# Weight blocks of K and Q loaded in joint pieces at the start of a one-core attention and feed-forward kernel

## The chip, the core and the metric

The kernel runs on one core of a Trainium2 chip. The metric is the device time of one execution in microseconds (us). The kernel before has a median of 210.56 us over 3 runs, which lie between 210.55 and 210.59 us.

## The reference

Input `x` has 2048 rows (tokens) of 512 numbers in bf16. The result is the sum of the input, a linear attention block and a feed-forward block, both applied to the normalised input:

```python
xn = _layernorm(x, axis=-1)
return x + _A_ref(xn, A_wqkv, A_wo) + _B_ref(xn, B_w_gate, B_w_up, B_w_down)

# A: qkv = xn @ wqkv (512 x 1536), 32 heads of 16
phi = lambda t: jnp.where(t > 0, t + 1, jnp.exp(t)) + 1e-6
pq, pk = phi(q), phi(k)
kv = einsum("bhsd,bhse->bhde", pk, v); z = einsum("bhsd->bhd", pk)
o = einsum("bhqd,bhde->bhqe", pq, kv) / (einsum("bhqd,bhd->bhq", pq, z)[..., None] + 1e-6)
# then o @ wo (512 x 512)
# B: (silu(xn @ w_gate) * (xn @ w_up)) @ w_down, inner width 1792
```

`wqkv` is one matrix of 512 rows and 1536 columns: columns 0 to 511 make Q, 512 to 1023 make K and 1024 to 1535 make V. So one row of it holds Q's 1 KB of weights directly ahead of K's 1 KB.

## The kernel before, in words

**Tiles.** The 2048 tokens are 16 tiles of 128. The width of 512 is 4 blocks (c = 0 to 3) of 128, since TensorE (PE) sums over 128 at a time. So K of one tile is four products, one per block of `xcT` (the centred input, transposed) and of the weights, summed in one bank of PSUM; `wk` c and `wq` c name the weights of block c for K and Q. A product of 128 x 128 by 128 x 512 is called a product below.

**Order.** Nothing is planned by a tool: the program is a list per engine, written out by hand, and every engine does its list in order. A helper (`_Prog`) records for each tile name who wrote it last, and adds the semaphore waits. A DMA signals when it has landed whole; every reader of any part of it waits for that. Loads are issued by SyncE (SP) and ScalarE (ACT), each from its own queue of DMAs; an ACT load stands in the same list as ACT's arithmetic.

**The start.** PE is kept running with five products of constants. Tiles 0 and 1 are transposed on PE raw (`traw`) and their mean is taken off there by a further product (`tcorr`); tile 0's mean comes from half sums (`sum_dve`, L388) in the kernel before already, and stays so. Tile 2 is centred on VectorE (DVE; `bns`, `agg`, two `xc_half`), transposed on PE (`tp_first`), and copied out by ACT (`tc_first`). Tile 3 is centred on DVE (`xc_full`) and transposed by a DMA (`transpose_xc`). The division by the standard deviation comes later, as a scale in ACT's `first_ek` (exponential of K), `first_pk` (positive part of K) and `first_pq` (Q).

**K and Q of tiles 0 and 1** (`proj_part`, L543) are written out product by product, in an order that follows the arrival of the weight blocks. K of tile 0 lies in bank 0, its Q in bank 1, K of tile 1 in bank 2, its Q in bank 3. Tile 2's `proj_first` (L530) uses banks 0 and 1 again and so waits for ACT's reads of them; tile 3 does with banks 2 and 3. ACT's list at this place is: `first_ek(0)`, `first_pk(0)`, `xn_act(0)`, two `tc_first(2)`, `first_pq(0)`, `first_ek(1)`, `first_pq(1)`, `first_pk(1)`. DVE's list is: `bns(2)`, `agg(2)`, two `xc_half(2)`, `bns(3)`, `agg(3)`, `clip_k(0)`, `xc_full(3)`, `bns(4)` and on with the statistics of tiles 5 and 6.

**After that** tiles 4 to 15 run in a loop (K, Q, their features, and the product of `xn` with the features of K, `gtacc`, L668), and then the feed-forward block (L870), with the output of four tiles worked in for each quarter of it (L1064, L1075).

**Loads of the start, before.** SP issues x 0, wk 0 and 1 (one DMA), wk 2, x 2, wq 0, wq 1, x 3, wq 2 and 3 (one DMA), x 4 and 5, x 6 and 7. ACT issues x 1 and wk 3. All weight loads read rows of 1 KB; x 4 and 5, and x 6 and 7, read rows of 2 KB, as there a partition takes two neighbouring tokens. A tile of x and a weight block are 128 KB each.

Of the kernel before, what the change touches and what calls it, by code (L numbers as in the profile page):

```python
# [10 lines left out]
P = 128  # L11
S = 2048
D = 512
# [96 lines left out]
def bass_parallel_sum__linear_attn_block__swiglu_ffn__prompt_kernel(  # L110
# [12 lines left out]
    K = _Prog()  # L123
    pe, act, dve, pool, sp = nc.tensor, nc.scalar, nc.vector, nc.gpsimd, nc.sync
    bf, f32 = dt.bfloat16, dt.float32

    with contextlib.ExitStack() as es:
        E = es.enter_context

        def sb(name, shape, d=bf):  # L130
            return E(nc.sbuf_tensor(name, [P] + shape, d))
# [7 lines left out]
        wqkv_sb = sb("wqkv_sb", [NDC, 3 * D])  # L139
# [16 lines left out]
        warm = sb("warm", [1], f32)  # L156
# [38 lines left out]
        def bk(i):  # L195
            return ("bank", i)
# [5 lines left out]
        def rows(v, t0, n):  # L202
            if t0 < NLONE:
                return v[t0 * P:(t0 + n) * P, :].rearrange("(t p) d -> p t d", p=P)
            return v[NLONE * P:, :].rearrange("(p t) d -> p t d", t=NT - NLONE)[:, t0 - NLONE:t0 - NLONE + n, :]

        def xload(eng, h, t0, n, after=()):
            K.dma(
                eng, lambda: h.dma_start(x_sb[:, t0:t0 + n, :], rows(xin, t0, n)),  # L209
                r=list(after), w=[("x", t0 + i) for i in range(n)],  # L210
            )

        def wqkv_load(eng, h, name, i, c0, n, after=()):
            K.dma(
                eng,
                lambda: h.dma_start(  # L216
                    wqkv_sb[:, c0:c0 + n, i * D:(i + 1) * D],
                    A_wqkv[c0 * P:(c0 + n) * P, i * D:(i + 1) * D].rearrange("(c p) f -> p c f", p=P),
                ),
                r=list(after), w=[(name, c) for c in range(c0, c0 + n)],  # L220
            )

        def wload(eng, h, name, dst, src):
            K.dma(eng, lambda: h.dma_start(dst[:, :, :], src.rearrange("(c p) f -> p c f", p=P)), w=[(name,)])

# [26 lines left out]

        xload("sp", sp, 0, 1)
        wqkv_load("sp", sp, "wk", 1, 0, 2)
        wqkv_load("act", act, "wk", 1, 3, 1)
        wqkv_load("sp", sp, "wk", 1, 2, 1)
        xload("sp", sp, 2, 1)
        wqkv_load("sp", sp, "wq", 0, 0, 1)
        wqkv_load("sp", sp, "wq", 0, 1, 1)
        xload("sp", sp, 3, 1)  # L260
        wqkv_load("sp", sp, "wq", 0, 2, 2)
        xload("sp", sp, 4, 2)
        xload("sp", sp, 6, 2)

# [34 lines left out]
        def bns(t):  # L299
            K.op("dve", lambda: dve.bn_stats(stats[:, t, :], x_sb[:, t, :]), r=[("x", t)], w=[("st", t)])  # L300

        def agg(t):
            K.op("dve", lambda: dve.bn_aggr(mv[:, t, :], stats[:, t, :]), r=[("st", t)], w=[("mv", t)])
# [155 lines left out]
        def tcopy(t, c0, n, b, eng):  # L459
            src, dst = banks[b][:, 0:n * P].rearrange("p (c s) -> p c s", c=n), xcT[:, NDC * t + c0:NDC * t + c0 + n, :]  # L460
            r, w = [bk(b)], [("xcT", t, c0 + i) for i in range(n)]
            if eng == "act":
                K.op("act", lambda: act.activation(dst, src, ACT.Copy), r=r, w=w)
            else:
                K.op("dve", lambda: dve.tensor_copy(dst, src), r=r, w=w)
# [10 lines left out]
        def transpose_xc(t):  # L476
            K.dma(
                "sp",
                lambda: sp.dma_start_transpose(out=xcT[:, NDC * t:NDC * (t + 1), :], in_=xc_sb[:, t, :]),
                r=[("xc", t, 0), ("xc", t, 1)], w=[("xcT", t, c) for c in range(NDC)],  # L480
            )
# [43 lines left out]
        def proj_first(t, wname, h):  # L525
            lo, b = (D, kb(t)) if wname == "wk" else (0, qb(t))
            K.op(
                "pe",
                [
                    (lambda c=c: pe.matmul(  # L530
                        banks[b], xcT[:, NDC * t + c, :], wqkv_sb[:, c, lo:lo + D],
                        start=(c == 0), stop=(c == NDC - 1),
                    ))
                    for c in (2 * h, 2 * h + 1)
                ],
                r=[("xcT", t, i) for i in (2 * h, 2 * h + 1)] + [(wname, i) for i in (2 * h, 2 * h + 1)], w=[bk(b)],
            )

        def proj_part(t, wname, c, pos):
            lo, b = (D, kb(t)) if wname == "wk" else (0, qb(t))  # L540
            K.op(
                "pe",
                lambda: pe.matmul(  # L543
                    banks[b], xcT[:, NDC * t + c, :], wqkv_sb[:, c, lo:lo + D],
                    start=(pos == 0), stop=(pos == NDC - 1),
                ),
                r=[("xcT", t, c), (wname, c)], w=[bk(b)],
            )

        def kb(t):  # L550
            return 2 * (t % 2)

        def qb(t):
            return 2 * (t % 2) + 1
# [43 lines left out]
        def first_ek(t):  # L598
            K.op(
                "act", lambda: act.activation(ek[:, t % NE, :], banks[kb(t)], ACT.Exp, scale=rstd[:, t:t + 1]),  # L600
                r=[bk(kb(t)), ("rstd", t)], w=[("ek", t % NE)],
            )

        def first_pk(t):
            K.op(
                "act", lambda: act.activation(kpos[:, t % NE, :], banks[kb(t)], ACT.Relu, scale=rstd[:, t:t + 1]),
                r=[bk(kb(t)), ("rstd", t)], w=[("kpos", t % NE)],
            )
# [7 lines left out]
        def first_pq(t):  # L616
            K.op(
                "act", lambda: act.activation(pkq[:, t, 1, :], banks[qb(t)], ACT.Identity, scale=rstd[:, t:t + 1]),
                r=[bk(qb(t)), ("rstd", t)], w=[("pq", t)],
            )  # L620
# [100 lines left out]
        proj_part(0, "wk", 1, 1)  # L721
        tcorr(1, 2, 3)
        tcopy(1, 2, 2, 3, "act")
        proj_part(0, "wk", 3, 2)
        proj_part(0, "wk", 2, 3)
        first_ek(0)
        clip_k(0)
        xc_full(3)
        bns(4)
        proj_part(1, "wk", 0, 0)  # L730
        proj_part(1, "wk", 1, 1)
        proj_part(1, "wk", 3, 2)
        proj_part(1, "wk", 2, 3)
        proj_part(1, "wq", 0, 0)
        proj_part(1, "wq", 1, 1)
        transpose_xc(3)
        xload("sp", sp, 8, 2)
        xload("sp", sp, 10, 2)
        proj_part(0, "wq", 0, 0)
        proj_part(0, "wq", 1, 1)  # L740
        first_pk(0)
        xn_act(0)
        tp_first(2, 0, 4)
# [5 lines left out]
        agg(5)  # L749
        bns(6)  # L750
        agg(6)
        proj_part(0, "wq", 2, 2)
        proj_part(1, "wq", 2, 2)
        proj_part(0, "wq", 3, 3)
        first_pq(0)
        proj_part(1, "wq", 3, 3)
        proj_first(2, "wk", 0)
        proj_first(2, "wk", 1)
        eps_two(1, "pool")
# [63 lines left out]
        for t in range(5, NT):  # L823
            kproj(t)
            exp_k(t)
            qproj(t)
            exp_q(t)
            copy_q(t)
            for i in XN0.get(t, ()):
                xn(i)  # L830
            feat_k(t)
            for i in STAT.get(t, ()):
                stat(i)
            for i in XN.get(t, ()):
                xn(i)
            if t in (6, 7, 8, 9):
                transpose_dma((3, 0, 1, 2)[t - 6])
            if t == 10:
                whalf("wg", wg_sb, B_w_gate, 0)
                whalf("wu", wu_sb, B_w_up, 0)  # L840
                wqkv_load("sp", sp, "wv", 2, 0, 4)
                wload("sp", sp, "wo", wo_sb, A_wo)
                whalf("wg", wg_sb, B_w_gate, 1)
            if t in (11, 12, 13, 14):
                late_eq(t - 11)
            if t == 12:
                masks()
            if t >= 12:
                gtacc(t - 2)
            elif t < 11:  # L850
                gtacc(t - 1)
# [260 lines left out]
        z_cols()  # L1112
        whalf("wu", wu_sb, B_w_up, 1)
        wload("sp", sp, "wd", wd_sb, B_w_down)
        NORM0 = 9
        PE_OUT = {3: 0, 6: 1, 9: 2, 12: 3}
# [56 lines left out]
```

## Time and profile before

| | before |
|---|---|
| median of 3 runs | 210.56 us (210.55 to 210.59) |
| the profiled execution | 210.56 us |
| its span, first to last instruction | 209.3 us |
| lies around the span | 1.26 us |
| PE busy | 205.0 us, 98% of the span |
| DVE, ACT, POOL busy | 119.7, 71.8, 72.2 us |
| granted TensorE clock | 1.00 |

All terms below come from this one profiled execution; its time is that of the median. Times are counted from the start of the span. A row of the timeline holds start, duration, engine, line, operation, output<-input and count; in brackets stands the idle time ahead of it and who ended it. "SPq" and "ACTq" are DMA issues; their duration is that of the issue, not of the transfer. "PEld" is PE's loading of the 128 x 128 operand, ahead of the product. A product is shown with 379 ns, but back-to-back ones start every 216 ns, since they overlap.

### The profile page before, as it was taken

The page shows a single profiled execution, that of the slowest core. Times are in us where ns is not written, and L with a number is a line of the kernel's source. Part 1 is how long each engine was busy: PE and PEld are TensorE (multiplying, and loading weights), DVE is VectorE, ACT ScalarE, POOL GpSimd, SP SyncE. Part 2 cuts the span into 40 slices and gives each one's busy share as a digit, 9 for nine tenths or more (in the row PEclk, how much of TensorE's full clock was granted, in tenths as well). Part 3 has the DMA queues.
Part 4 walks back from the last instruction along what each step waited for, and adds up shares of the span by engine and source line. Part 5 has one row for each costly group of instructions (what it writes and reads, how often), then busy time and mean ns, then how long its engine had stood idle before and what let it go on. Part 6 is the DMA issues. An engine that isn't in the chain of part 4 may idle for free.

```text
span 209.3 us, 2809 instructions
## 1 busy us (share of the span) xinstructions
PE 205.0 (98%) x998; PEld 94.5 (45%) x1017; DVE 119.7 (57%) x245; ACT 71.8 (34%) x127; POOL 72.2 (34%) x91
## 2 busy tenths in 40 slices
PE   8999999999999999999999999999999999999996
PEld 4444444444444444444444444444444444444444
DVE  4799988336365874637355746365556545374122
ACT  6877666966643331312112312213031213121000
POOL 2537987668032543223041422240424132221200
PEclk9999999999999999999999999999999999999999
DMA  6765645894696011010201110102011010110201
GB/s 197 219 184 79 127 100 102 258 364 153 206 356 49 11 39 25 28 25 25 52 0 50 28 28 22 50 0 53 5 45 25 25 28 28 49 27 27 53 25 50
DMA packets 30127, 16.84 MB, mean 80 GB/s; under 512 B 20896, under 2 KB 29344, under 8 KB 30112
## 3 DMA queue, kind: packets, MB, share of 16 engines
q1 hardware_dynamic: 29824, 16.39, 30.0%
q10 hardware_dynamic: 288, 0.26, 0.4%
q8 instruction: 8, 0.13, 0.2%
q14 instruction: 7, 0.06, 0.1%
HBM read 9.70 MB, written 2.10 MB: 56 GB/s over the span
## 4 chain that ended last, share of the span: by engine, by line
PE 91%; DVE 3%; DMA 2%; SPq 1%; issue 1%; POOL 1%; DVEq 0%
PE psum L870 44%; PE psum L1075 23%; PE psum L516 9%; PE psum L1064 7%; PE psum L668 6%; DMA wqkv_sb<-in_A_wqkv_dram 2%; PE psum L530 2%; SPq L216 1%; DVE pkq L592 1%; SPq L209 1%; POOL prod L1019 1%; PE psum L543 0%; DVE xn_sb L317 0%; DVE den L1027 0%; DVE pkq L891 0%
## 5 line engine op out<-in xcount | busy, mean ns | idle before, releaser
L885 ACT ACTIVATE sg<-psum 128x512 bf16<-128x512 f32 x56 | 33.4, 599 | 106.0 <-PE psum L870 103.6
L870 PE MATMUL psum<-xnT,wg_sb 128*128 128x512 bf16 x222 | 57.2, 379 | 0.2 <-issue 0.2
L870 PE MATMUL psum<-xnT,wu_sb 128*128 128x512 bf16 x216 | 55.8, 379 | 0.4
L1019 POOL TENSOR_TENSOR prod<-pkq,zb 128x512 f32<-128x512 bf16 x16 | 18.6, 1163 | 55.9 <-DVE pkq L592 55.9
L870 PEld LDWEIGHTS psum<-xnT,wu_sb 128*128 128x128 bf16 x224 | 21.9, 98 | 26.4
L870 PEld LDWEIGHTS psum<-xnT,wg_sb 128*128 128x128 bf16 x224 | 21.7, 98 | 26.2 <-issue 0.2
L1088 DVE TENSOR_TENSOR out_sb<-psum,x_sb 128x512 bf16<-128x512 f32 (+2 forms) x17 | 11.2, 661 | 36.2 <-PE psum L1075 36.2
L1043 POOL TENSOR_TENSOR pqn<-pkq,rden 128x512 bf16<-128x512 bf16 x16 | 16.9, 1058 | 36.6 <-DVE rden L1037 36.6
L891 DVE TENSOR_TENSOR pkq<-psum,sg 128x512 bf16<-128x512 f32 x28 | 19.2, 686 | 17.1 <-PE psum L870 14.6
L891 DVE TENSOR_TENSOR xn_sb<-psum,sg 128x512 bf16<-128x512 f32 x28 | 18.8, 672 | 13.8 <-PE psum L870 13.3
L1075 PE MATMUL psum<-wd_sb,xn_sb 128*128 128x512 bf16 (+2 forms) x126 | 25.7, 355 | 0.0
L1075 PE MATMUL psum<-wd_sb,pkq 128*128 128x512 bf16 x108 | 25.1, 379 | 0.2
L516 PE MATMUL psum<-wqkv_sb,xnT 128*128 128x512 bf16 x95 | 22.5, 379 | 0.1
L660 POOL TENSOR_TENSOR zacc<-zacc,pkq 128x512 f32<-128x512 f32 x15 | 17.4, 1157 | 5.0 <-DVE ek L583 4.6
L1075 PEld LDWEIGHTS psum<-wd_sb,xn_sb 128*128 128x128 bf16 x126 | 11.8, 98 | 12.5
L1075 PEld LDWEIGHTS psum<-wd_sb,pkq 128*128 128x128 bf16 x112 | 11.0, 98 | 13.2
L1064 PE MATMUL psum<-m_sb,eq 128*128 128x512 bf16 (+2 forms) x67 | 16.4, 366 | 0.1
L668 PE MATMUL psum<-pkq,xn_sb 128*128 128x512 bf16 x61 | 15.6, 379 | 0.2
L516 PEld LDWEIGHTS psum<-wqkv_sb,xnT 128*128 128x128 bf16 x96 | 9.4, 98 | 11.3
L1027 DVE TENSOR_REDUCE den<-prod 128x32 f32<-128x512 f32 x16 | 10.9, 684 | 5.9 <-POOL prod L1019 5.9
L300 DVE BATCH_NORM_STATS2 stats<-x_sb 128x6 f32<-128x512 bf16 x16 | 10.9, 680 | 1.1 <-DMA x_sb<-in_A_x_dram 1.1
L592 DVE SCALAR_TENSOR_TENSOR pkq<-pkq,eq 128x512 bf16<-128x512 bf16 x16 | 11.1, 692 | 0.6
(78 smaller groups left out, 139.7 us busy)
## 6 DMA issues: line engine op xcount, KB each, us to landing
out_dram<-out_sb SPq DMA_DIRECT2D x15, 128.0 KB, 1.7
wg_sb<-in_B_w_gate_dram SPq DMA_DIRECT2D x2, 896.0 KB, 7.5
wu_sb<-in_B_w_up_dram SPq DMA_DIRECT2D x2, 896.0 KB, 5.9
wd_sb<-in_B_w_down_dram SPq DMA_DIRECT2D x1, 1792.0 KB, 11.1
x_sb<-in_A_x_dram SPq DMA_DIRECT2D x6, 256.0 KB, 3.2
wqkv_sb<-in_A_wqkv_dram SPq DMA_DIRECT2D x2, 256.0 KB, 3.6
wqkv_sb<-in_A_wqkv_dram SPq DMA_DIRECT2D x1, 512.0 KB, 7.7
wo_sb<-in_A_wo_dram SPq DMA_DIRECT2D x1, 512.0 KB, 8.7
```

The lines of the kernel that those rows point to most:

```text
L516: (lambda c=c: pe.matmul(banks[b], xnT[:, c, t * P:(t + 1) * P], wqkv_sb[:, c, lo:lo + D], start=(c == 0), stop=(c == NDC - 1),))
L592: lambda: dve.scalar_tensor_tensor(out=dst, in0=src, scalar=0.0, in1=e, op0=ALU.max, op1=ALU.add,),
L660: lambda: pool.tensor_tensor(out=zacc[:, :], in0=zacc[:, :], in1=pk, op=ALU.add),
L668: (lambda c=c: pe.matmul(banks[4 + c], xn_sb[:, t, c * P:(c + 1) * P], pkq[:, t, 0, :], start=(t == 0), stop=(t == NT - 1),))
L870: (lambda c=c: pe.matmul(banks[b], w_sb[:, c, fc * P:(fc + 1) * P], xnT[:, c, C * 512:(C + 1) * 512], start=(c == 0), stop=(c == NDC - 1),))
L885: lambda: act.activation(sg[:, j % NSG, :], banks[gb], ACT.Silu),
L891: lambda: dve.tensor_tensor(out=hT(C, fc), in0=banks[ub], in1=sg[:, j % NSG, :], op=ALU.mult,),
L1019: lambda: pool.tensor_tensor(out=p, in0=pkq[:, t, 1, :], in1=zb[:, :], op=ALU.mult),
L1043: lambda: pool.tensor_tensor(out=pqn[:, t % NPN, :].rearrange("p (i g h e) -> p g i h e", i=NB, g=NG, e=DH), in0=pkq[:, t, 1, :].rearrange ...
L1064: (lambda g=g: pe.matmul(dst, pqnT(t)[:, g, :], m_sb[:, g, lo:hi], start=(g == 0), stop=False,))
L1075: (lambda fc=fc: pe.matmul(dst, hT(C, fc)[:, jj * P:(jj + 1) * P], wd_sb[:, fc, lo:hi], start=False, stop=(fc == NFC - 1),))
L1088: lambda: dve.tensor_tensor(out=o, in0=src, in1=x_sb[:, t, lo:hi], op=ALU.add),
```

## The change

A new function `qk_load` reads one block's rows over columns 0 to 1023, so Q's and K's weights of that block come in one DMA of 256 KB, in rows of 2 KB. It is used for blocks 2 and 3. Blocks 0 and 1 stay as they were for K (one DMA), and Q's blocks 0 and 1 become one DMA, issued behind x 3. The load of x 2 goes from SP's to ACT's queue, with a wait for ACT's first activation (`warm`); wk 3 leaves ACT's queue. Loads of the start are 10 in place of 12, with the same bytes.

The products of tiles 0 and 1 are put in another order: K of tile 0 takes blocks 0, 1, 2, then tile 1's K takes blocks 0 and 1, then tile 0's block 3 closes its K, then tile 1's blocks 2 and 3. Q takes blocks 2 and 3 of both tiles first and blocks 0 and 1 last. Their number is the same.

```diff
+        def qk_load(eng, h, c):
+            K.dma(
+                eng,
+                lambda: h.dma_start(wqkv_sb[:, c, 0:2 * D], A_wqkv[c * P:(c + 1) * P, 0:2 * D]),
+                w=[("wk", c), ("wq", c)],
+            )
...
         xload("sp", sp, 0, 1)
         wqkv_load("sp", sp, "wk", 1, 0, 2)
-        wqkv_load("act", act, "wk", 1, 3, 1)
-        wqkv_load("sp", sp, "wk", 1, 2, 1)
-        xload("sp", sp, 2, 1)
-        wqkv_load("sp", sp, "wq", 0, 0, 1)
-        wqkv_load("sp", sp, "wq", 0, 1, 1)
+        xload("act", act, 2, 1, [("warm",)])
+        qk_load("sp", sp, 2)
+        qk_load("sp", sp, 3)
         xload("sp", sp, 3, 1)
-        wqkv_load("sp", sp, "wq", 0, 2, 2)
+        wqkv_load("sp", sp, "wq", 0, 0, 2)
         xload("sp", sp, 4, 2)
         xload("sp", sp, 6, 2)
...
         proj_part(0, "wk", 1, 1)
         tcorr(1, 2, 3)
         tcopy(1, 2, 2, 3, "act")
-        proj_part(0, "wk", 3, 2)
-        proj_part(0, "wk", 2, 3)
+        proj_part(0, "wk", 2, 2)
+        proj_part(1, "wk", 0, 0)
+        proj_part(1, "wk", 1, 1)
+        proj_part(0, "wk", 3, 3)
+        proj_part(1, "wk", 2, 2)
+        proj_part(1, "wk", 3, 3)
         first_ek(0)
         clip_k(0)
         xc_full(3)
         bns(4)
-        proj_part(1, "wk", 0, 0)
-        proj_part(1, "wk", 1, 1)
-        proj_part(1, "wk", 3, 2)
-        proj_part(1, "wk", 2, 3)
-        proj_part(1, "wq", 0, 0)
-        proj_part(1, "wq", 1, 1)
+        proj_part(0, "wq", 2, 0)
+        proj_part(0, "wq", 3, 1)
         transpose_xc(3)
         xload("sp", sp, 8, 2)
         xload("sp", sp, 10, 2)
-        proj_part(0, "wq", 0, 0)
-        proj_part(0, "wq", 1, 1)
+        proj_part(1, "wq", 2, 0)
+        proj_part(1, "wq", 3, 1)
         first_pk(0)
...
-        proj_part(0, "wq", 2, 2)
-        proj_part(1, "wq", 2, 2)
-        proj_part(0, "wq", 3, 3)
+        proj_part(0, "wq", 0, 2)
+        proj_part(0, "wq", 1, 3)
+        proj_part(1, "wq", 0, 2)
         first_pq(0)
-        proj_part(1, "wq", 3, 3)
+        proj_part(1, "wq", 1, 3)
```

## The prediction

> **What bounds the kernel now.** I read the page's busy times first, then PE's waits, the chain of work that ended last, and then the first 16 us of the timeline.
>
> ```profile
> PE 205.0 (98%) x998; PEld 94.5 (45%) x1017; DVE 119.7 (57%) x245; ACT 71.8 (34%) x127; POOL 72.2 (34%) x91
> ...
> PE psum L543 <- DMA wqkv_sb<-in_A_wqkv_dram: 0.5, 1, 0.5
> PE psum L870 <- issue: 0.2, 1, 0.2
> ...
> 4.12 4.19 DMA wqkv_sb<-in_A_wqkv_dram
> 8.36 1.04 PE psum L543 x4
> ```
>
> PE is the bound. Once it has begun at 8.36 us it goes on back to back to the end, but for 0.2 us; the only wait before that worth a name is 0.5 us for a weight DMA, wq 2 and 3, issued at 4.12. So the change moves the end by as much as it moves PE's unbroken run, and by any new stall that it puts into the run. It cannot gain much more than the 0.5 us: ahead of 8.36 PE is busy.
>
> The loads that set that start, in order of issue (SP's, then ACT's with the activation `warm`):
>
> ```profile
> 0.80 0.40 SPq L209 DMA_DIRECT2D x_sb<-in_A_x_dram  x1
> 1.26 0.92 SPq L216 DMA_DIRECT2D wqkv_sb<-in_A_wqkv_dram  x2
> 2.23 0.43 SPq L209 DMA_DIRECT2D x_sb<-in_A_x_dram  x1
> 2.70 0.91 SPq L216 DMA_DIRECT2D wqkv_sb<-in_A_wqkv_dram  x2
> ...
> 4.12 0.44 SPq L216 DMA_DIRECT2D wqkv_sb<-in_A_wqkv_dram  x1
> ...
> 1.10 0.42 ACTq L209 DMA_DIRECT2D x_sb<-in_A_x_dram  x1
> 1.56 0.45 ACTq L216 DMA_DIRECT2D wqkv_sb<-in_A_wqkv_dram  x1
> 2.09 0.20 ACT L239 ACTIVATE warm<-warm 128x1 f32<-128x1 f32 x1
> ```
>
> And the instructions that date the landings: the first product is the first to use wk 3, the second to use wk 2; the others were released by a landing. The last row is of the view of the weights' tile for the issue at 1.26 alone: wk 0 and 1 land 3.0 us on, at 4.26.
>
> ```profile
> 5.28 2.36 PE L543 MATMUL psum<-wqkv_sb,xcT 128*128 128x512 bf16 x10
> 6.08 0.69 DVE L300 BATCH_NORM_STATS2 stats<-x_sb 128x6 f32<-128x512 bf16 x1 [0.76 <-DMA x_sb<-in_A_x_dram]
> 6.45 0.10 PEld L543 LDWEIGHTS psum<-wqkv_sb,xcT 128*128 128x128 bf16 x1 [0.21 <-DMA wqkv_sb<-in_A_wqkv_dram]
> 6.82 0.33 PEld L543 LDWEIGHTS psum<-wqkv_sb,xcT 128*128 128x128 bf16 x3 [0.27 <-DMA wqkv_sb<-in_A_wqkv_dram]
> 8.36 0.55 PEld L543 LDWEIGHTS psum<-wqkv_sb,xcT 128*128 128x128 bf16 x4 [0.67 <-DMA wqkv_sb<-in_A_wqkv_dram]
> 9.15 0.69 DVE L300 BATCH_NORM_STATS2 stats<-x_sb 128x6 f32<-128x512 bf16 x1 [0.38 <-DMA x_sb<-in_A_x_dram]
> DMA to landing us min/median/max: 3.0/3.0/3.0
> ```
>
> The five landings between are x 2, wq 0, wq 1, wq 2 and 3, and x 4 and 5. With 128 KB for a block or tile, so many bytes had been asked for up to and with each: 512 KB at 4.26 us, 896 at 6.08, 1024 at 6.45, 1152 at 6.82, 1536 at 8.36, 1792 at 9.15. Loads land in order of issue, 3 to 4.5 us after it, and the interval between landings is set by bytes, not by the 0.46 us between issues.
>
> **The change, part by part.**
>
> *Bytes.* They are the same. What changes is the order and the piece. The cost of a piece, from the DMA view of 4.5 to 6.5 us (nearly all 1 KB pieces) and of 7.5 to 8.5 us (nearly all 2 KB):
>
> ```profile
> DMA packets 668, 0.62 MB, mean 308 GB/s; under 512 B 67, under 2 KB 667, under 8 KB 668
> ...
> q1 hardware_dynamic: 667, 0.62, 101.3%
> ...
> DMA packets 180, 0.32 MB, mean 321 GB/s; under 512 B 18, under 2 KB 29, under 8 KB 180
> ...
> q1 hardware_dynamic: 180, 0.32, 86.0%
> ```
>
> The first is 1.013 x 16 engines x 2 us = 32.4 engine-us for 600 pieces, 54 ns each (completion packets taken as free). The second is 0.86 x 16 x 1 = 13.8 for 162 pieces; less 11 of 54 ns, 87 ns for each of 151. So 2 KB cost 87 ns in place of 108. The change turns 512 KB, 512 pieces, into 256: 256 x 21 ns / 16 engines = 0.34 us. I take g = 0.3 us. Its ends are 0 and 0.7 us. 0, because a landing waits for the slowest engine, not for the mean one, and in landings 128 KB of 1 KB pieces took 0.37 us (6.45 to 6.82), 256 KB of 2 KB pieces 0.79 us (8.36 to 9.15), no faster. 0.7, because the 512 KB from 4.26 to 6.45 took 2.19 us, against 4 x 0.37 = 1.48 at that pace: the rest is delay, and whether it comes again with other pieces no row tells. 0.3 is the mean engine's value and near the middle.
>
> The Trainium skill, page "Perfetto Trace Analysis", section "DMA Optimizations", says that DMAs under 2 KB have significant overhead each and larger ones use the memory better; here that is 108 against 87 ns for 2 KB, so the trace agrees in direction, and the sum takes the row's size. The same section says that splitting a load may let work start sooner, which speaks against this change: see wk 3 next.
>
> *Order of landing.* After the change SP issues x 0, wk 0 and 1, qk 2, qk 3, x 3, wq 0 and 1, x 4 and 5, x 6 and 7, at the pace above: 0.80, 1.26, 1.73, 2.2, 2.7, 3.1, 3.6, 4.1. ACT issues x 1 at 1.10 and x 2 once `warm` has ended (2.09 + 0.20), at about 2.35, between qk 3 and x 3. The issue takes ACT's queue 0.4 us, as wk 3's did before, at a time when ACT waits for x 1 to land: it costs nothing. Placed by bytes: qk 3 ends at 1024 KB, where before stood 6.45; x 2 at 1152 KB (6.82); wq 0 and 1 at 1536 (8.36); x 4 and 5 at 1792 (9.15). Less g: **qk 3 6.15, x 2 6.52, the last weights 8.06, x 4 and 5 8.85**. So the last weights come 0.3 us sooner, but wk 3, whose product with wk 2's closed tile 0's K from 5.28 on, is about 0.9 us later, and x 2 0.44 us later.
>
> *What is behind these.* The rows, by engine, the last of the view of DMA issues (us from issue to landing):
>
> ```profile
> 7.48 0.39 PE L488 MATMUL psum<-ident,xc_sb 128*128 128x128 bf16 x4
> 7.37 0.32 PEld L488 LDWEIGHTS psum<-ident,xc_sb 128*128 128x128 bf16 x4 [0.22 <-DVE xc_sb L381]
> 11.70 0.23 PEld L530 LDWEIGHTS psum<-wqkv_sb,xcT 128*128 128x128 bf16 x2 [0.20 <-ACT kpos L606]
> 14.25 0.70 PEld L668 LDWEIGHTS psum<-pkq,xn_sb 128*128 128x128 bf16 x4 [0.17 <-DVE pkq L632]
> 5.91 0.69 ACT L600 ACTIVATE ek<-psum,rstd 128x512 bf16<-128x512 f32 x1
> 7.79 0.66 ACT L500 ACTIVATE xcT<-psum 128x256 bf16<-128x256 bf16 x2
> 9.22 0.69 ACT L618 ACTIVATE pkq<-psum,rstd 128x512 bf16<-128x512 f32 x1 [0.77 <-PE psum L543]
> 9.81 0.68 ACT L600 ACTIVATE ek<-psum,rstd 128x512 bf16<-128x512 f32 x1
> 7.03 0.48 DVE L381 TENSOR_SCALAR xc_sb<-x_sb,mv 128x256 bf16<-128x256 bf16 x2
> 8.42 0.35 DVE L470 TENSOR_SCALAR xc_sb<-x_sb,mv 128x512 bf16<-128x512 bf16 x1
> 7.48 0.72 POOL L354 TENSOR_TENSOR rstd<-vpe,nhalf 128x2 f32<-128x2 f32 x1
> 8.79 1.29 SPq L479 DMA_TRANSPOSE xcT<-xc_sb  x1
> xcT<-xc_sb SPq DMA_TRANSPOSE x1, 2.5
> ```
>
> PE: after 5.28 it has three products (tile 0's block 2, tile 1's blocks 0 and 1), to 5.93, and waits for qk 3 until 6.25 (with 0.1 for the operand). Seven products of 0.216 us follow, to 7.76; then tile 2's four transposes, which need x 2: `bns(2)` at 6.52, `xc_half` 0.95 us on at 7.47 (6.08 to 7.03 above), operand at 7.81 (7.03 to 7.37), transposes 7.92 to 8.3. Then the last four products of Q at 8.31, against 8.36: PE gains 0.05.
>
> ACT: before, tile 0's K closes with the second product after 5.28, at 5.50, and `first_ek(0)` starts 0.41 later. After: 6.25 + 0.41 = 6.66. From there ACT runs without a break through `first_pk(0)`, `xn_act(0)` and the two copies; before that was 5.91 to 8.45, 2.54 us. So `first_pq(0)` can start at 9.20, against 9.22 before, where ACT had 0.77 us to spare: the change uses up that spare time. What is queued behind it is tight: PE's operand load at 11.70 waits for `first_pk(1)`, the fourth of ACT's list from there, and PE's run has no gap at that place.
>
> DVE: from `bns(2)` at 6.08 to the end of `xc_full(3)` at 8.77 it is a chain of 2.69 us without a wait, then 0.38 us of idle until x 4. From 6.52 it ends at 9.21. So `bns(4)` starts at 9.21, not when x 4 and 5 land (8.85), and not at 9.15: 0.06 late. DVE goes on without a break, and at 14.25 PE's operand load waits for it (`first_feat(2)`), again with nothing to spare. SP's transposing DMA of tile 3 is queued behind `xc_full(3)` and goes 0.44 us later: it lands at 8.79 + 2.5 + 0.44 = 11.73, and PE wants it with the operand load at 11.70. So its cover is just used up; each 0.1 us more of x 2 would be 0.1 us of stall here. Behind it on SP stand the loads of x 8 to 11, whose tiles DVE reaches only after tile 3's features. POOL's `rstd` of tiles 1 and 2 comes 0.44 us later than its 8.20, at 8.64, and `first_ek(1)` uses it at 9.81: hidden by 1.2 us.
>
> *Sum.* PE -0.05, ACT -0.02, DVE +0.06; the latest sets the run: **+0.05 us**, 210.56 + 0.05 = 210.6.
>
> **Rivals.**
>
> *B: x 2 overtakes qk 3.* ACT's queue may be served beside SP's. Between 3.5 and 4.0 us both moved data, wk 3 (issued at 1.56 by ACT) beside wk 0 and 1 (issued at 1.26):
>
> ```profile
> q1 hardware_dynamic: 101, 0.09, 56.2%
> q10 hardware_dynamic: 98, 0.10, 55.8%
> ```
>
> Against it: wk 3 did not start before then, though x 1 was through, so the order of issue ruled. If it overtakes, qk 3 ends at 1152 KB: 6.82 - 0.3 = 6.52, `first_ek(0)` at 7.03, `first_pq(0)` at 9.57, 0.35 late: **210.9**; with g = 0, 211.2. It is slower whenever qk 3 lands after 6.17 (9.22 - 2.54 - 0.51).
> The Trainium skill, page "DMA: Bandwidth & Descriptors", section "Queues, rings and completion order", has each DMA engine take turns between the rows that have work; by that rule this rival holds. The rows at 3.5 to 4.0 agree, the late start of wk 3 does not.
>
> *C: the 2 KB pieces save nothing at the slowest engine* (g = 0). qk 3 at 6.45 makes ACT 0.28 late, x 2 at 6.82 makes DVE 0.74 - 0.38 = 0.36 late: **210.9**, and 211.2 where one engine holds back qk 3 by 0.3 us more, since K of tile 0 hangs on one landing.
>
> *D: faster.* If the pace of 0.37 us for 128 KB holds from 4.26 on, qk 3 lands at 5.74 and x 2 at 6.11. Then ACT is 0.43 us early, and DVE's chain from x 2 ends at 8.8, so that `bns(4)` gains 0.35 us if x 4 is there: **210.2**. For it: the interval from 6.08 to 6.82 did keep that pace. Against: the 384 KB from 6.82 to 8.36 took 1.54 us, not 1.11; delays came before and after.
>
> **How the numbers follow.** The forecast (g from 0.1 to 0.5: qk 3 at 6.35 to 5.95, x 2 at 6.7 to 6.3, 210.4 to 210.85) has 0.45; B 0.22, C 0.2, D 0.13. The 8 in 10 range takes D's end and the late ends of B and C: 210.15 to 211.2. What can be told from no change is 0.2%, 0.42 us. Slower than 210.98 are about half of B and C and some stall I have not seen, 0.3; faster than 210.14 is D's better half and a little of the forecast's, 0.15; within, 0.55.
>
> **What would show it.** In the changed kernel: PE idle near 6 us for qk 3 and hardly any at 8.3; `first_ek(0)` near 6.7 and no idle ahead of `first_pq(0)`; `bns(2)` near 6.5 and `bns(4)` without idle ahead of it; the landing of wq 0 and 1 no later than 8.1. Wrong would be a `first_ek(0)` beyond 7.0, x 2 landing before qk 3, a wait on the transposed tile 3 at 11.8, or PE stalls after 10 us that none of these rows leads to.

## The result and the profile after

The changed kernel takes 211.5 us (median of 13 runs, 211.04 to 212.11), the kernel before 210.75 (13 runs, 210.45 to 211.19): a ratio of 1.0035, 95% interval 1.0024 to 1.0046. It is slower by 0.75 us, where 210.6 and no measurable change had been forecast. Measured again with the experiments, the same kernel took 211.26 against 210.94, a ratio of 1.0011 (0.9999 to 1.0023). So the loss is clear in the first measurement; in the second it is smaller, and its interval just takes in no change. Where single profiles are read below, that is to be kept in mind.

The profiled run of the changed kernel is its slowest, 212.11 us with a span of 210.9; before had 210.56 and 209.3. The profile thus shows 1.6 us of loss, twice the loss of the medians; I read it as a bad instance of the same mechanism. The page's busy times and PE's waits, and the start of the chain that ended last (start, length, what):

```profile
PE 206.6 (98%) x1017; PEld 94.3 (45%) x1017; DVE 119.6 (57%) x245; ACT 71.6 (34%) x127; POOL 72.0 (34%) x91
...
PE psum L548 <- DMA wqkv_sb<-in_A_wqkv_dram: 1.6, 1, 1.6
...
PEld psum L535 <- ACT kpos L611: 0.3, 1, 0.3
...
1.73 5.55 DMA wqkv_sb<-in_A_wqkv_dram
7.41 2.34 PE psum L548 x10
10.84 1.85 PE psum L535 x8
13.55 1.73 PE psum L535 x8
```

Before, the one wait was 0.5 us for the last weights, issued at 4.12. Now it is 1.6 us for qk 2, issued at 1.73, and the wait for the last weights is gone. PE's timeline of the changed kernel from 5 us:

```profile
5.53 0.27 PE L457 MATMUL psum<-dg,const-bfloat16-1.0 128*128 128x256 bf16 x1
7.41 2.34 PE L548 MATMUL psum<-wqkv_sb,xcT 128*128 128x512 bf16 x10 [1.62 <-DMA wqkv_sb<-in_A_wqkv_dram]
9.59 0.39 PE L493 MATMUL psum<-ident,xc_sb 128*128 128x128 bf16 x4
9.81 1.03 PE L548 MATMUL psum<-wqkv_sb,xcT 128*128 128x512 bf16 x4
10.79 1.90 PE L535 MATMUL psum<-wqkv_sb,xcT 128*128 128x512 bf16 x8
12.53 1.03 PE L673 MATMUL psum<-pkq,xn_sb 128*128 128x512 bf16 x4
13.39 1.89 PE L535 MATMUL psum<-wqkv_sb,xcT 128*128 128x512 bf16 x8
```

I use the last row as a marker: the eight products of tile 3's K. They began at 11.82 in the kernel before and at 13.39 here, 1.57 us later, which is the difference of the spans: behind the marker both kernels take 197.5 us. So the whole loss lies ahead of the marker. The rows behind the landings, by engine:

```profile
8.06 1.19 PEld L548 LDWEIGHTS psum<-wqkv_sb,xcT 128*128 128x128 bf16 x7 [0.34 <-DMA wqkv_sb<-in_A_wqkv_dram]
10.79 0.11 PEld L535 LDWEIGHTS psum<-wqkv_sb,xcT 128*128 128x128 bf16 x2 [0.44 <-ACT xcT L505]
13.37 0.55 PEld L535 LDWEIGHTS psum<-wqkv_sb,xcT 128*128 128x128 bf16 x4 [0.31 <-ACT kpos L611]
2.33 0.34 ACTq L209 DMA_DIRECT2D x_sb<-in_A_x_dram  x1
8.50 0.69 ACT L605 ACTIVATE ek<-psum,rstd 128x512 bf16<-128x512 f32 x1 [2.28 <-PE psum L548]
10.88 0.70 ACT L623 ACTIVATE pkq<-psum,rstd 128x512 bf16<-128x512 f32 x1
12.59 0.73 ACT L611 ACTIVATE kpos<-psum,rstd 128x512 f32<-128x512 f32 x1
7.52 0.69 DVE L305 BATCH_NORM_STATS2 stats<-x_sb 128x6 f32<-128x512 bf16 x1 [2.14 <-DMA x_sb<-in_A_x_dram]
10.15 0.69 DVE L305 BATCH_NORM_STATS2 stats<-x_sb 128x6 f32<-128x512 bf16 x1
1.73 0.94 SPq L226 DMA_DIRECT2D wqkv_sb<-in_A_wqkv_dram  x2
```

The operand load at 8.06 was released by qk 3: it landed at about 8.0, not at 6.15. `first_ek(0)` follows 0.4 later at 8.50, not at 6.66. From there ACT goes without a gap through `first_pq(0)` (10.88) to `first_pk(1)` (12.59). PE's operand loads wait for that list, first at 10.79 for ACT's copy of tile 2 (`tc_first(2)`) and last at 13.37 for `first_pk(1)`. But PE is late by itself, too. From 7.41 to the marker the starts of its products stand 0.22 us apart (the four transposes take as long as one product), with one longer step, 0.33 us, at 10.79. So ACT delayed PE by 0.11 us there and nowhere else; with an ACT that was never late, PE would have reached the marker at 13.28, still 1.46 us late. x 2 landed at 7.5, ahead of qk 3, though ACT issued it at 2.33, 0.1 us after SP's issue of qk 3.

The DMA view of the changed kernel from 5.0 to 5.5 us (packets, MB, share of the 16 engines; q10 is ACT's queue) shows how:

```profile
q1 hardware_dynamic: 63, 0.10, 63.1%
q10 hardware_dynamic: 70, 0.07, 39.0%
```

Both queues move data at once: x 2 shares the engines with the loads that SP issued before it. And the completions that the trace records for each of the 16 engines show that a landing is the last of 16. For qk 2, fifteen engines were done by 5.23 and the last at 7.28; for qk 3, eight by 5.78, fifteen by 7.06, the last at 8.02; for x 2, eight by 5.95, the last at 7.50. So in the middle of the list qk 3 was still a little ahead of x 2, and at its end x 2 came first.

### The profile page after: what moved, and what is told of

The parts are those of the page before. It is cut to its first block, busy times and chain, and to the rows that moved or that the text cites. A ratio compares the mean times of both kernels' runs of the same rounds, so it can differ in the third digit from the quotient of the medians.

```text
span 210.9 us, 2826 instructions
## 1 busy us (share of the span) xinstructions
PE 206.6 (98%) x1017; PEld 94.3 (45%) x1017; DVE 119.6 (57%) x245; ACT 71.6 (34%) x127; POOL 72.0 (34%) x91
## 4 chain that ended last, share of the span: by engine, by line
PE 96%; DMA 3%; SPq 0%; issue 0%; DVE 0%
PE psum L875 46%; PE psum L1080 23%; PE psum L521 10%; PE psum L1069 7%; PE psum L673 7%; DMA wqkv_sb<-in_A_wqkv_dram 3%; PE psum L535 2%; PE psum L548 2%; PE psum L982 0%; SPq L216 0%; SPq L209 0%; PE psum L1005 0%; DVE out_sb L1093 0%; PE psum L493 0%
## 5 line engine op out<-in xcount | busy, mean ns | idle before, releaser
L875 PE MATMUL psum<-xnT,wu_sb 128*128 128x512 bf16 x224 | 57.5, 379 | 0.0
```

What stands on the lines that cost most here:

```text
L875: (lambda c=c: pe.matmul(banks[b], w_sb[:, c, fc * P:(fc + 1) * P], xnT[:, c, C * 512:(C + 1) * 512], start=(c == 0), stop=(c == NDC - 1),))
```

## The experiments

The theory after the result: tile 0's K closes with qk 3. It is asked for behind 1024 KB, and with x 2 taking turns it lands behind 1152 KB; PE stands still for K's blocks, and from `first_ek(0)` on ACT has no spare time left either. Rivals: the late x 2 through DVE; the 2 KB pieces; the order of the products; the clock. Each kernel was timed against the kernel before on the same chip.

**Which of the moved loads costs?** First the changed kernel again, as the level for the others.

> The changed kernel unchanged, for a second profile and the spread. Three theories of the 0.75 us. P (pieces): loads in 2 KB pieces that begin while the queues are full stall for most of a us on some engines, and tile 0's K hangs on two such loads. O (order): the pieces do not matter, wk 3 simply stands behind 1024 KB in place of 768 KB. X (queue): x 2 on ScalarE's queue takes turns with qk 3 and pushes it back. All expect 211.3 to 211.7 here. P expects the first product on block 2 or 3 late again (6.8 us or later) with most of the delay at engines that stalled; O and X expect about 6.5 to 6.9 and the 8.0 of the first profile to be chance.

Measured: 211.26 us (13 runs) against 210.94 before, 1.0011 (0.9999 to 1.0023). The loss of 0.32 us is below the 0.75 of the first measurement, and by itself it is not told from no change. Its profiled run was one of 213.3 us; of that below, under the clock.

`x2_on_sp` puts x 2 back on SP's queue, behind qk 3:

```
-        xload("act", act, 2, 1, [("warm",)])
         qk_load("sp", sp, 2)
         qk_load("sp", sp, 3)
+        xload("sp", sp, 2, 1)
         xload("sp", sp, 3, 1)
```

> The changed kernel with x 2 back on SyncE's queue, between qk 3 and x 3; nothing else differs. X expects a gain of 0.3 to 0.4 us over the changed kernel (211.1 to 211.2), since qk 3 then ends 128 KB sooner. P and O expect 211.3 to 211.7, no difference beyond 0.15 us.

Measured: 210.8 us, 0.9993 (0.9981 to 1.0005) of before, 0.46 us less than `after_again`. With one queue qk 3 landed at 6.5 and x 2 after it, at 7.0. In its timeline (PE, ACT, DVE, SP):

```profile
6.55 1.68 PE L548 MATMUL psum<-wqkv_sb,xcT 128*128 128x512 bf16 x7 [0.31 <-DMA wqkv_sb<-in_A_wqkv_dram]
12.41 1.89 PE L535 MATMUL psum<-wqkv_sb,xcT 128*128 128x512 bf16 x8
6.97 0.69 ACT L605 ACTIVATE ek<-psum,rstd 128x512 bf16<-128x512 f32 x1 [0.96 <-PE psum L548]
7.02 0.69 DVE L305 BATCH_NORM_STATS2 stats<-x_sb 128x6 f32<-128x512 bf16 x1 [1.43 <-DMA x_sb<-in_A_x_dram]
9.76 1.30 SPq L484 DMA_TRANSPOSE xcT<-xc_sb  x1
```

Here K is nearly early enough, and it is x 2 that sets the marker in this one execution: SP's transposing DMA starts at 9.76, and 9.76 + 2.5 is 12.26, behind the 11.82 at which PE began before. That is the wait on the transposed tile 3 that the prediction named. So taking x 2 off ACT's queue takes the loss away in the medians. Single landings vary too much to show it (see `after_fill`).

`k_first` keeps x 2 on ACT but asks for K's two blocks as one load of 1 KB pieces, ahead of Q's two:

```
-        qk_load("sp", sp, 2)
-        qk_load("sp", sp, 3)
+        wqkv_load("sp", sp, "wk", 1, 2, 2)
+        wqkv_load("sp", sp, "wq", 0, 2, 2)
```

> The changed kernel with wk 2 and 3 in one load of 1 KB pieces, then wq 2 and 3 in one, so that K's last block closes at 768 KB and x 2 stands behind it. O expects a gain of 0.6 to 0.8 us (210.6 to 210.9). P expects the same gain, since no 2 KB piece is left in K's way, so against pieces_1k it tells what the order is worth without 2 KB pieces: P about 0 to 0.2 us, O 0.6 or more. X expects a gain of half that or less.

Measured: 210.75 us, 0.9997 (0.9983 to 1.0011); `first_ek(0)` at 6.96 and the marker at 11.98 in its profile. With K early, x 2 may stay on ACT's queue at no cost that these runs can tell. (K's blocks had landed at 5.08 in this profile; `first_ek(0)` waited until 6.96 for PE, whose starts at 4.68, 5.11, 5.53, 5.75 and 6.11 stand up to 0.43 us apart.)

`pieces_1k` keeps the order in bytes but uses 1 KB pieces, in four loads, with K's last block at the end:

```
-        qk_load("sp", sp, 2)
-        qk_load("sp", sp, 3)
+        wqkv_load("sp", sp, "wk", 1, 2, 1)
+        wqkv_load("sp", sp, "wq", 0, 2, 1)
+        wqkv_load("sp", sp, "wq", 0, 3, 1)
+        wqkv_load("sp", sp, "wk", 1, 3, 1)
```

> The changed kernel with qk 2 and qk 3 each loaded as two loads in 1 KB pieces, in the order wk 2, wq 2, wq 3, wk 3, so that wk 3 still closes 1024 KB. P expects most of the loss gone: 210.7 to 211.0, first exponential of K near 6.9 us. O and X expect it to stay: 211.3 to 211.8 (two more issues, and the mean engine 0.3 us slower by the row of 108 against 87 ns).

Measured: 211.33 us, 1.0016 (1.0003 to 1.003), against 211.26 for the 2 KB pieces. Twice the pieces cost nothing that these runs can tell, though the two intervals are too wide to rule out the 0.3 us of g. The Trainium skill, page "Perfetto Trace Analysis", section "DMA Optimizations", which the prediction weighed, has overhead in pieces under 2 KB; these runs don't show it in the time.

`x2_first` moves x 2 on ACT's queue directly behind x 1. It lands before the weights, and K still closes behind 1152 KB:

```
-        xload("act", act, 2, 1, [("warm",)])
+        xload("act", act, 2, 1, [("nhalf",)])
```

> The changed kernel with x 2 issued on ScalarE's queue directly behind x 1 (it waits for the same memset as x 1, not for the first activation), so that x 2 lands before qk 2 and qk 3, which then close 1152 KB as in the changed kernel. Two theories of what the late blocks cost. K: the landing of tile 0's last K block sets the time, through ScalarE's list; x 2 has cover. Z: x 2's landing sets it, through VectorE's chain and the transposed tile 3. K expects no gain over the changed kernel: 211.1 to 211.5. Z expects 210.7 to 210.9.

Measured: 210.97 us against 210.68, 1.0012 (1.0000 to 1.0024): +0.29, about the loss of `after_again` (+0.32); the interval begins at no change. x 2 landed at 6.42 in its profile, inside its spare time, and qk 3 at 7.21, so the lateness of x 2 is not what costs; K's is. (This profile, too, has the clock drop, below.)

`x2_sp_ahead` gives that order to one queue: x 2 on SP, between qk 2 and qk 3.

```
-        xload("act", act, 2, 1, [("warm",)])
         qk_load("sp", sp, 2)
+        xload("sp", sp, 2, 1)
         qk_load("sp", sp, 3)
```

> The changed kernel with x 2 on SyncE's queue between qk 2 and qk 3, so that tile 0's last K block closes 1152 KB, as it does in the changed kernel by x 2 taking turns, but with one queue only. Two readings of what x 2 on ScalarE's queue costs. Bytes: the 128 KB that get ahead of qk 3 are all; then this kernel loses as much as the changed kernel with x 2 first did, 0.25 to 0.45 us against before (211.0 to 211.2). Queue: two queues at once slow the transfers (254 to 281 GB/s from 4 to 5 us in the profiles with x 2 on ScalarE's queue behind the activation, 312 to 345 without); then this kernel loses 0.15 us or less (210.6 to 210.9).

Measured: 211.06 us against 210.68, +0.38 by the medians; the ratio, 1.0007 (0.9987 to 1.0028), does not tell it from no change, so this run alone decides nothing, nor between its two readings. (The 254 to 281 GB/s of the second reading leave out `pieces_1k`, which moved 202.) Its PE and ACT rows agree with the theory: qk 3 behind 1152 KB landed at 7.44, without any load on ACT's queue beside it.

```profile
7.49 1.68 PE L548 MATMUL psum<-wqkv_sb,xcT 128*128 128x512 bf16 x7 [0.34 <-DMA wqkv_sb<-in_A_wqkv_dram]
12.81 1.89 PE L535 MATMUL psum<-wqkv_sb,xcT 128*128 128x512 bf16 x8
7.91 0.69 ACT L605 ACTIVATE ek<-psum,rstd 128x512 bf16<-128x512 f32 x1 [1.50 <-PE psum L548]
```

**Does the order of the products cost?** `both_undone` keeps the new order of products and takes both moves of loads back: K's blocks first, then x 2 on SP, then Q's.

```
-        xload("act", act, 2, 1, [("warm",)])
-        qk_load("sp", sp, 2)
-        qk_load("sp", sp, 3)
+        wqkv_load("sp", sp, "wk", 1, 2, 2)
+        xload("sp", sp, 2, 1)
+        wqkv_load("sp", sp, "wq", 0, 2, 2)
```

> The changed kernel's order of products, with both suspects undone: wk 2 and 3 in one load ahead (768 KB), then x 2 on SyncE's queue (896 KB), then wq 2 and 3, x 3, wq 0 and 1. All bytes stand where the kernel before has them. K and Z expect 210.6 to 210.95, the time of the kernel before: the new order of the products and Q's blocks 0 and 1 last cost nothing. If the order of the products costs by itself, 211.1 or more.

Measured: 210.59 us, 0.9998 (0.9988 to 1.0008). The new order of products costs nothing that these runs can tell. It doesn't help measurably either.

**The same two moves in the kernel before.** `x2_act_only` moves only x 2 to ACT's queue; `x2_for_wk3` exchanges x 2 and wk 3 between the queues:

```
-        xload("sp", sp, 2, 1)
+        xload("act", act, 2, 1, [("warm",)])
```

```
-        wqkv_load("act", act, "wk", 1, 3, 1)
-        wqkv_load("sp", sp, "wk", 1, 2, 1)
-        xload("sp", sp, 2, 1)
+        xload("act", act, 2, 1, [("nhalf",)])
+        wqkv_load("sp", sp, "wk", 1, 2, 2)
```

> The kernel before with one part of the change: x 2 on ScalarE's queue with the wait for the first activation, behind wk 3. K's blocks are all ahead of it. K expects the time of the kernel before within 0.15 us (210.7 to 211.0). Z expects the same or a little better, 210.6 to 210.9, if x 2 lands sooner than 6.1 us; if ScalarE's queue by itself costs something, 211.1 or more.

> The kernel before with x 2 and wk 3 exchanged: x 2 on ScalarE's queue directly behind x 1, wk 2 and 3 in one load on SyncE's. x 2 lands before 5.2 us, tile 0's K closes 896 KB near 6.0 us. K expects first_ek(0) near 6.5 us, inside the 0.77 us that ScalarE had to spare ahead of first_pq(0): 210.7 to 211.0. Z expects a gain, since VectorE's chain starts 0.8 us sooner: 210.4 to 210.7.

Measured: 210.66 us, 1.0004 (0.999 to 1.0017), and 210.62 us, 1.0009 (0.9988 to 1.0031). Neither shows a loss, though the second interval reaches 0.6 us up. So no harm is seen from x 2 on ACT's queue while K's last block ends at 896 KB or less.

**Is ACT the way by which it costs?** `act_pad1` and `act_pad2` put one and two extra copies, whose results nobody reads, ahead of `first_ek(0)` in the kernel before. No load is moved.

```
+        def act_pad():
+            K.op("act", lambda: act.activation(scr[:, :], x_sb[:, 0, :], ACT.Copy), r=[("x", 0)], w=[("scr",)])
...
+        act_pad()
         first_ek(0)
```

> The kernel before with one copy of a tile (about 0.6 us, its output is not used) put into ScalarE's list ahead of first_ek(0), so that this list starts that much later with no load touched. The step on ScalarE's spare time says that 0.77 us ahead of first_pq(0) cover it: 210.6 to 210.8, no loss beyond 0.15 us. If ScalarE's list has no such cover, 0.6 us slower: 211.2 or more.

> The same with two copies, about 1.2 us, as late as a last K block near 6.7 to 7.0 us makes the list in the changed kernel. The step on ScalarE's list says that what goes beyond the spare time delays the run one to one: 0.3 to 0.5 us slower than before, 211.0 to 211.2. If nothing there is tight, no change; if late K blocks hurt through PE or VectorE instead, no change either.

Measured: 210.64 us, 0.9994 (0.9985 to 1.0002), and 210.89, 1.0008 (0.9997 to 1.0018), +0.17 by the medians, which is not told from no change. ACT's timeline with two copies:

```profile
7.04 0.67 ACT L600 ACTIVATE ek<-psum,rstd 128x512 bf16<-128x512 f32 x1
9.41 0.70 ACT L618 ACTIVATE pkq<-psum,rstd 128x512 bf16<-128x512 f32 x1
11.12 0.73 ACT L606 ACTIVATE kpos<-psum,rstd 128x512 f32<-128x512 f32 x1
```

`first_ek(0)` is 1.13 us later than before (5.91). `first_pq(0)` starts 2.37 us on, without a gap, 0.19 later than its 9.22. The list back to back is 2.37 us, not the 2.54 that the prediction read off the kernel before, and the spare time is 9.22 - 2.37 - 5.91 = 0.94 us. That accounts for a smaller cost than expected. What goes beyond the spare time shows in the marker (11.92, 0.10 later): PE waited at 9.32 for ACT's copy of tile 2, as in the changed kernel. So the pads show how much lateness ACT's list takes; that it is the later path in the changed kernel is read from the rows, by 0.11 us.

**Can PE's idle time be the cost?** `after_fill` puts three products of constants ahead of qk 2's first product and one ahead of qk 3's, so that PE doesn't idle; nobody reads them.

```
+        fill6(3)
         proj_part(0, "wk", 2, 2)
         proj_part(1, "wk", 0, 0)
         proj_part(1, "wk", 1, 1)
+        fill6(1)
         proj_part(0, "wk", 3, 3)
```

> The changed kernel with three products of constants ahead of tile 0's K block 2 and one ahead of its block 3 (a spare bank; nothing reads it), so that PE is not idle for 1.5 us at a stretch. Twice a profile of a kernel that waited so showed the granted clock at 0.5 for 3.4 us behind the wait, and 212.1 or 211.8 us of span. If the wait brings that drop, this kernel shows no run of 211.9 us or more among some 13, and a median of 210.8 to 211.3, that of the changed kernel or a little less. If the drops come by chance, one or two such runs stay.

Measured: 211.58 us (7 runs), 1.0032 (1.002 to 1.0045). One of the seven was over the 211.9 of the expectation (212.09). It doesn't recover the loss: qk 3 landed at 6.34 in this profile, ahead of x 2 (6.54), but the inserted products held PE until 7.59, and `first_ek(0)` came at 8.00. So it delayed K by itself, and what it does for the clock can't be told from it.

**All profiles by one rule.** The prediction's two paths, with ACT's list corrected, say how late the marker is: by ACT, `first_ek(0)` + 2.37 - 9.22; by DVE and SP, x 2's first instruction - 6.52 (its 0.44 us of spare time). The larger counts, and a negative one counts nothing. Every number is a start in the profiles:

```
                 first_ek(0)  x 2   by ACT  by x 2   marker   later than 11.82
changed             8.50     7.52    1.65    1.00     13.39     1.57
x2_sp_ahead         7.91     6.82    1.06    0.30     12.81     0.99
pieces_1k           7.91     6.89    1.06    0.37     12.80     0.98
after_fill          8.00     6.57    1.15    0.05     12.90     1.08
x2_for_wk3          7.22     6.07    0.37     -       12.42     0.60
x2_on_sp            6.97     7.02    0.12    0.50     12.41     0.59
x2_act_only         5.95     6.87     -      0.35     12.20     0.38
k_first             6.96     6.60    0.11    0.08     11.98     0.16
act_pad2            7.04     5.58    0.19     -       11.92     0.10
both_undone         6.54     6.24     -       -       11.60    -0.22
```

Nine of the ten agree within 0.1 us, if the -0.22 of the last is put down to the wait for the last weights (0.5 us before), which it doesn't have. The odd one is `x2_for_wk3`, 0.23 too late, and it points at a third path that the rule leaves out, PE's own. Its rows:

```profile
6.59 2.32 PE L542 MATMUL psum<-wqkv_sb,xcT 128*128 128x512 bf16 x10 [1.01 <-DMA wqkv_sb<-in_A_wqkv_dram]
9.83 1.89 PE L529 MATMUL psum<-wqkv_sb,xcT 128*128 128x512 bf16 x8
12.42 1.89 PE L529 MATMUL psum<-wqkv_sb,xcT 128*128 128x512 bf16 x8
```

K's blocks landed at 6.45, PE began at 6.59 and went without a gap to its marker at 12.42, so PE alone makes its 0.60. In `x2_sp_ahead`, `pieces_1k` and `after_fill` it is as in the changed kernel: from tile 0's last block of K to the marker PE has one gap of 0.11 us, at ACT's copy of tile 2. So the first four rows of the table fit PE's own path nearly as well as ACT's, 0.11 us short of the marker. A K that comes late costs on both paths at once, and relieving ACT alone would have saved 0.11 us in these profiles.

`act_pad1` belongs to neither path: the last weights came 0.40 later (8.76 for 8.36), its marker 0.41. The two profiles at a lower clock stand apart.

## Why the prediction was wrong

*What bounds the kernel: right.* PE runs unbroken from its last wait on, and behind the marker nothing moved.

*The order of landing: wrong; this is the step that failed.* "Placed by bytes: qk 3 ends at 1024 KB" takes the queues for one line in order of issue. Rival B's condition held instead: x 2, issued 0.1 us after qk 3 on the other queue, took turns with it. qk 3 landed at 8.02 in the first profile and 7.66 in the second, after x 2 both times (7.50 and 7.10), instead of 6.15. In `after_fill`, a third profile with the same loads, it landed at 6.34, ahead of x 2: which of the two ends first varies, and single landings don't give the price. The medians do. The Trainium skill, page "DMA: Bandwidth & Descriptors", section "Queues, rings and completion order", says that an engine goes round the queues that have work; the rows from 5.0 to 5.5 us agree. The late start of wk 3 in the kernel before, for which I had set that rule aside, did not carry over to x 2. Where K ends at 1152 KB (the changed kernel, `x2_first`, `pieces_1k`, `x2_sp_ahead`), the medians are 0.29 to 0.75 us over before; where K ends at 768 to 1024 KB (`x2_on_sp`, `k_first`, `both_undone`, `x2_act_only`, `x2_for_wk3`), they lie between 0.19 under and 0.02 under it.

*The saving of the pieces, g = 0.3 us: not seen.* `pieces_1k` shows no difference, though it can't rule out 0.3. Two things speak for less. The row's 54 and 87 ns are shares of busy time, with a few long packets in them; in the records of single packets 1 KB takes 46 ns and 2 KB 84 ns in the median, so that two small pieces cost 8 ns more than a large one, not 21, which is 0.13 us on the mean engine. And a landing waits for the last engine, the reason that I had named for my lower end, 0. With g = 0, rivals B and C hold together: B was then worked out at 211.2, against a measured 211.5 and, in the second measurement, 211.26.

*Bounds of a landing: too narrow.* I took the landings of one profile as a pace. How far the last engine is behind the fifteenth changes from load to load and from execution to execution: 0.03 us for wk 2 in the kernel before (5.05 and 5.08), 2.05 us for qk 2 in the changed kernel's first profile. Of the 1.57 us there, up to 0.96 is the last engine of qk 3, if that of qk 2 had been in time as well: fifteen had their share of qk 3 by 7.06, the last at 8.02. The kernel before can meet such accidents too (0.50 us between the last two engines of x 2), but its K is asked for earlier, and ACT's 0.94 us are there to cover them.

*ACT: right, but for the size of its spare time* (0.94, not 0.77 us). The chain from `first_ek(0)` on is the one in the rows, PE meets it first at the copy of tile 2 and then at `first_pk(1)`, and the padded kernels show its cover without any load being moved. It is the latest of the paths in the changed kernel, but by 0.11 us alone.

*DVE and x 2: right in mechanism, not what decided.* bns(4) follows without idle time (10.15), and the wait for the transposed tile 3 came where x 2 was late and K was not (`x2_on_sp`, 0.59 us in the marker).

*PE: the order of the products right, the -0.05 us wrong.* The wait for the last weights is gone and nothing else came of the order (`both_undone`). But the -0.05 was worked out with qk 3 used at 6.25 and with qk 2 there by 5.28, for which the prediction gave no landing. qk 2 landed at 7.28 and 6.92 in the two profiles, and PE's own path was 1.46 us late in the first of them.

What stays open: the size. The same kernel lost 0.75 us on one occasion and 0.32 on another, and I can't say how much of the difference is the spread of the slowest engine and how much the clock (next).

None of the variants is shown to be faster than the kernel before; the intervals of the two lowest ratios, of `act_pad1` and `x2_on_sp`, take in no change.

## What to carry to other kernels

A load moved to a second queue to start it earlier takes its share from the loads already under way: place it against what they release, not only against its own use. For a product that closes a chain, ask for its last operand early and count the spare time behind it on every engine that goes on from there, the one that waits included, since the landing is that of the slowest of 16 engines; and a saving read as a mean over the engines is no saving of a landing. A path's spare time is best measured by padding it, which here corrected 0.77 to 0.94 us.

## What the runs showed that I had not expected

The granted clock of PE can fall after a short idle time. In the profiled runs of `after_again` (213.3 us) and `x2_first` (212.99 us) PE had waited about 1.5 us for weights; the ten products after that took 4.00 us where they take 2.34. PE's row, and the windows of `after_again` (window, length, then busy time of the engines, granted clock, DMA share, GB/s):

```profile
7.05 4.00 PE L548 MATMUL psum<-wqkv_sb,xcT 128*128 128x512 bf16 x10 [1.50 <-DMA wqkv_sb<-in_A_wqkv_dram]
...
7.00:8.00 1.00, 0.95 (x3) 0.33 (x4) 0.84 (x2) 0.00 (x0) 0.00 (x0) 0.67 1.06 403
8.00:10.00 2.00, 2.00 (x6) 0.76 (x5) 1.87 (x8) 1.28 (x3) 1.05 (x2) 0.50 0.24 90
10.00:11.00 1.00, 1.00 (x5) 0.41 (x4) 0.97 (x3) 0.68 (x1) 0.94 (x1) 0.63 0.00 0
```

That is 1.7 us lost in such a run. The first profile of the changed kernel had 1.62 us of the same wait and kept a clock of 1.00, so the idle time doesn't decide alone. What differs ahead of the wait: there PE's last products before it started 0.43 us apart (4.74 and 5.17), in the other two 0.21, though the granted clock reads 1.00 in all three. The Trainium skill, page "TensorE: Matmul & The Clock Gate", section "Part 1: The HAM clock gate (the "warmup" mystery)", has the clock set by how busy PE was in a window of about 3.4 us that runs free of the kernel. In the windows above 0.33, 1.00 and 0.37 us of full clock are missing, which is 3.4 us at half clock and agrees with one such window, and that it runs free would explain why equal waits end differently; no run here tests that. Runs of this length are rare (one of 13, one of 14; one of 12 of `x2_for_wk3` and one of 17 of the kernel before reached 212.78 or more without a profile), so they hardly move a median.

A load's last engine can be far behind the others: for qk 2 in the changed kernel by 2.05 us (5.23 to 7.28). The records of single packets show one 2 KB packet that took 2.05 us there, where most take 0.084.
